# Layer two of an attention and mixture-of-experts kernel: how routing steps are let in between the products

## The chip, the cores and the metric

The kernel runs on one core of a Trainium2 chip. The metric is the time of one execution in device microseconds (us). A core has TensorE (PE, matrix products), VectorE (DVE), ScalarE (ACT), GpSimd (POOL), and the queue of SyncE (SP), which issues most transfers. Each engine takes its own instructions in order; between engines only semaphores order the work.

## The reference

Three stages follow each other, all in fp32. Stage one is attention (4 batches, 8 heads, 768 positions, 64 wide). Stage two sends each of 3072 tokens that a skip score keeps to its best of 8 experts. Stage three, called layer two here, is the one that the change touches:

```python
cap = N // E                                  # 3072 // 8 = 384
logits = x @ w_gate
for idx in np.argsort(-logits.flatten()):     # best pairs first
    tok, e = idx // E, idx % E
    if assigned[tok] >= 0 or counts[e] >= cap:
        continue
    assigned[tok] = e
    counts[e] += 1
for e in range(E):
    mask = assigned == e
    out[mask] = np.maximum(x[mask] @ w1[e], 0.0) @ w2[e]
```

So every expert gets 384 tokens, and which ones depends on which experts were full before.

## The kernel before, in words

**Products.** Layer two has eight units, one per expert, in the order in which the experts fill up. A unit works through 8 chunks of its 1024 hidden columns. Operands are split into a high and a low half (`xh`, `xl`, `wh`, `wl`, `h` twice), so that a chunk is 12 matmuls `ph` (128x384) and 9 matmuls `py` (128x512), 1344 in all. `wh` is written by ScalarE from the raw weights `wr` (four buffers, filled by SP), `wl` by POOL in four steps of 128x256, or by VectorE in one of 128x1024.

**Routing.** `phase` (line 1731) finds which expert fills next and which tokens it takes. It searches the threshold in 7 digits. For each digit VectorE compares all scores (`gm`), TensorE counts (`pr<-oh,gm`), and VectorE reads the digit off the counts. A count has two forms: the direct one (24 matmuls, then `fl,wt`) and the grouped one (six matmuls, a cast `cs`, then one or four sum matmuls with `sel` or `sels`; the last digit uses `identh` and `fl,wt`). Then follow `c,tri`, `ttb,tri`, `part,ones` and three `tb_rhs,mp`, each after VectorE operations; the last give the token numbers `ids`. With these POOL gathers the rows of the next unit (three gathers `xg`), TensorE turns them (`ident,xg`), ScalarE writes `xh` and VectorE `xl`. SP reads the expert's number `ei` and loads its weights.

**What sets the order.** The program is written out once, with a planner beside it. `Clock` (line 20) keeps a planned time for each engine; `cost` (line 76) says how long an operation is planned to take, and `ready` when an operand is planned to be there. The routing and the turns are generators (`Stream`, line 1211). Before each product `hook` (line 1240) lets a stream take its next step if `when()` is not later than the planned TensorE time plus `T_EPS`; `wait_for` (line 1258) steps the streams when there are no products, with matmuls on fixed data (`ph<-ones,tri`) as fill. The planner's numbers thus decide how many products stand between two routing steps in TensorE's queue, and nothing else: at run time the queues simply run.

**The start of layer two** (lines 2016 to 2034). Unit 0's rows are gathered in three blocks; `do_load` (line 508) puts a tiny write into the weight buffer ahead of each of four loads (the gate), so that the load can't start before that write has its turn. Meanwhile the fill runs, and phase 1 is already under way. `direct` (line 1757) says which digits are counted in the direct form, numbering them through the phases: the first 13.

Of the kernel before, what the change touches and what calls it, by code (L numbers as in the profile page):

```python
# [12 lines left out]
AF = mybir.ActivationFunctionType  # L13
# [6 lines left out]
class Clock:  # L20
# [4 lines left out]
    def __init__(self):  # L25
        self.at = dict.fromkeys(("pe", "dve", "act", "pool", "sp", "dma"), 0.0)
        self.seen, self.slots, self.count, self.log = {}, {}, {}, {}
        self.on = False
        self.late, self.fine = 0, False

    def place(self, t):
        if t.name not in self.slots:
# [43 lines left out]
    def cost(self, eng, op, outs, ins, extra):  # L76
        n = max([1] + [a.free_size() for a in outs[:1] + ins])
        if eng == "pe":
            d = str(ins[-1].dtype)
            n = outs[0].free_size()  # L80
            if op == "matmul" and d.endswith("float32") and ins[0].free_size() == 32 and outs[0].start_partition():
                n = 8
            if d.endswith("float32r") and ins[0].free_size() == 128:
                n = max(n, 250)
            return max(0.027, n * (2 if op == "transpose" else 4 if d.endswith("float32") else 1) / 2400.0)
        if eng == "dve":
            one = op in ("tensor_copy", "tensor_scalar", "memset") and all(a.tensor.space != "PSUM" for a in ins) and n % 2 == 0
            return 0.067 + 0.06 * extra + n / (1920.0 if one else 960.0)
        if eng == "act":
            return (0.051 if any("PSUM" in str(a.tensor.space) for a in ins) else 0.094) + n / 1200.0  # L90
        if op == "indirect_dma_start":
            return 1.038
        return 0.036 + n * (0.0022 if op == "tensor_tensor" else 0.0011)
# [77 lines left out]
def tile_attn_moe_moe(ctx: ExitStack, tc: tile.TileContext, q, k, v, n_global, n_local,  # L171
                      w_skip, w_gate, w1, w2, w2_gate, w21, w22, out):
    nc = Chip(tc.nc)
# [45 lines left out]
    pcol = sm.tile([128, 1], F32, name="pcol")  # L219
# [229 lines left out]
    class Weights:  # L449
# [58 lines left out]
        def do_load(self, i):  # L508
            c = self.order[i]
            u, j = divmod(c, NCH)  # L510
            t = wraw.tile([128, 1024], F32, name="wr")
            a = self.src[u][0 if j < 4 else 1]
            if self.gate:
                nc.vector.memset(t[0:1, 0:1], 0.0)
            if j < 4 and u in self.by_cols:
                nc.sync.dma_start(t.rearrange("p (c f) -> p c f", c=KC),
                                  a(0, Dm).rearrange("(c p) f -> p c f", p=128)[:, :, j * 256:(j + 1) * 256])
            elif j < 4:
                nc.sync.dma_start(t, a(j * 128, 128))
            else:  # L520
                nc.sync.dma_start(t.rearrange("p (c d) -> p c d", c=2),
                                  a((j - 4) * 256, 256).rearrange("(c p) d -> p c d", p=128))
            self.raw[c] = t
            self.loaded += 1
# [33 lines left out]
    WWT, WWN = 1, (2, 5)  # L558
    T_GAP, T_SP, T_EPS, T_W, T_P, T_L, T_F, X_B, T_H, T_M, LEAN, T_G, DIRECT, CUT = 0, 0.65, 0.1, 0, 8, 1, 0.3, 3, -4, 0, 2, 1, 13, 16
    T_LOW = 0.7  # L560
    LATE = 0.3
    PAUSE = 1
    T_U = 0.15
    ck.late = 2.0
# [293 lines left out]
    for g in range(-3, NU + 1):  # L858
# [16 lines left out]
        m, t = divmod(g + 4, NG)  # L875
# [35 lines left out]
    class Unit:  # L911
        at, tb, py, defer, xh, x2, turns, third, banks = None, 0, 0, None, None, None, False, False, None
        n = [128] * (CAP // 128)
# [294 lines left out]
    unit_no = [0]  # L1208
    result = {}

    class Stream:
# [12 lines left out]
        def when(self):  # L1224
            eng, aps = self.need
            if eng == "pt":
                t = ck.ready("pe", last_pt, aps)
                return max(t, ck.at["dve"] + T_LOW) if lows else t
            t = ck.ready(eng, (), aps)
            return max(t, ck.at["dve"] - T_SP) if eng == "dve" else t  # L1230

    streams = []
    held_back = []

    def order():
        free = [s_ for s_ in streams if not s_.busy]
        now = [s_ for s_ in free if not (s_.kind in held_back and s_.need[0] == "dve")]
        return sorted(now or free, key=lambda s_: s_.rank())
# [12 lines left out]
    def warm(until):  # L1251

        if ck.at["pe"] + 0.11 <= until:
            p = fps.tile([128, 512], F32, name="ph", bufs=2)
            while ck.at["pe"] + 0.11 <= until:
                nc.tensor.matmul(p[:, :256].rearrange("p (a n) -> p a n", a=2), tri, wide_one, start=True, stop=True)

    def wait_for(over, fill=False):
        while not over():
            t = min(s_.when() for s_ in order()) + T_F  # L1260
            s_ = next(s_ for s_ in order() if s_.when() <= t)
            if unit_no[0] < 0 and s_.kind == "main":
                first_ = min((o for o in order() if o.kind != "main"), key=lambda o: o.when(), default=None)
                if first_ and first_.when() < s_.when() + T_M:
                    s_ = first_
            if fill and s_.need[0] != "dve":
                warm(s_.when() - T_U)
            s_.step()
# [225 lines left out]
    BITS = ((27, 32), (22, 32), (17, 32), (12, 32), (7, 32), (2, 32), (0, 4))  # L1494
# [236 lines left out]
    def phase(ph_):  # L1731
# [7 lines left out]
        mb = m[:, :, None]  # L1739
        for it, (s_, n_) in enumerate(() if last else BITS):  # L1740
            if it and any(s_.kind == 'x' for s_ in streams):
                yield "dve", ()
            gm_ = rt.tile([128, NT * 32], BF, name="gm")
            gm = gm_[:, :NT * n_].rearrange("p (t n) -> p t n", n=n_)
            cut = {0: [CUT], 1: [2 * NT // 3]}.get(ph_, [])
# [7 lines left out]
            if it:  # L1753
                dv.tensor_tensor(nx[:, 0, :nn], tb_[:, :nn], thr[:, 0:1].to_broadcast([128, nn]),
                                 op=OP.bitwise_xor)
            low = it + 1 == len(BITS)
            direct = ph_ * len(BITS) + it < DIRECT
            wide = not direct and not low
            cnt = fps.tile([128, 2, 64], F32, name="pr")[:, 0, :CG * E]
            if direct:  # L1760
# [57 lines left out]
        else:  # L1818
            dv.scalar_tensor_tensor(fo[:, 0], pn_, v_[:, 1:2], first, op0=OP.is_equal, op1=OP.mult)
        dv.tensor_reduce(fx[:, 0:1], fo[:, 0], axis=AX.X, op=OP.max)  # L1820
        wait_for(lambda: not [s_ for s_ in streams if s_.kind == "ids"])
        yield "dve", ()
        fe = rt.tile([128, 6, NT], F32, name="fe", bufs=2)
        if not last:
            ts_ = thr.bitcast(F32)
# [90 lines left out]
    def routing():  # L1916
        yield from table_rows(units1[E - 1])
        for p in range(E):
            yield from phase(p)
# [74 lines left out]
    units2 = []  # L1994
# [21 lines left out]
    held_back.clear()  # L2016
    ck.late = LATE
    units2[0].banks = ("pt", "py1", "py2")
# [2 lines left out]
    split_next()  # L2021
    W_.gate = True
    for tb in range(1, NH):
        wait_for(lambda: units2[0].tb == tb, True)
        W_.limit = W_.limit + 1 if tb + 1 < NH else None
        W_.preload()
    W_.gate = False
# [38 lines left out]
```

## Time and profile before

| | before |
|---|---|
| median of 3 runs (lowest, highest) | 775.62 us (775.53, 776.88) |
| the profiled execution: time, span | 777.47 us, 775.7 us |
| TensorE busy in the span | 744.8 us (96%) |
| VectorE, ScalarE, POOL busy | 526.1, 403.3, 468.2 us |
| granted TensorE clock | 0.997 |
| stages: attention, layer one, start of layer two, layer two, end | 264.6, 185.9, 14.1, 305.6, 5.5 us |

The stages were cut at the first and last product of each. Busy time is that of the intervals in which an engine had an instruction in work. The end of a matmul is modelled in the profile, so rows of TensorE are read by their starts: from the start of one to the start of the next. The numbers in brackets behind a row of a timeline are the idle time of that engine ahead of it, and what ended it.

### The profile page before, as it was taken

Reading aid. Unit: us, or ns where it says so; the run is one execution under the profiler, and the core shown is the slowest. Engines: PE = TensorE matmul, PEld = TensorE weight load, DVE = VectorE, ACT = ScalarE, POOL = GpSimd, SP = SyncE. Lnnn points to the kernel's source line nnn. Section 1 sums busy time; section 2 is a strip of 40 time slices with the busy share of each in tenths; the row PEclk is TensorE's granted clock in tenths of the full one; section 3 lists DMA queues with packets and bytes.
Section 4 is the critical chain, followed back from the end, with each engine's and each line's share of the span. In section 5 each row is a group of like instructions: output and inputs, shape, how many; then the busy total and the mean of one; then the engine's idle time right before and its main releaser. Section 6 shows DMA issues by size and latency. Waiting matters only on the chain.

```text
span 775.7 us, 17432 instructions
## 1 busy us (share of the span) xinstructions
PE 744.8 (96%) x5910; PEld 628.7 (81%) x5910; DVE 526.1 (68%) x1952; ACT 403.3 (52%) x936; POOL 468.2 (60%) x821
## 2 busy tenths in 40 slices
PE   7999999899889999999999999999999999999997
PEld 5887777677659999999888677878788878788986
DVE  5987988979556676777634586778787778752110
ACT  5887787887547655555652113434333434255221
POOL 4664456755214464555793636975768777689911
PEclk9999999999999999999999999999999999999999
DMA  8686988897716766777760035626262636366311
GB/s 192 167 213 167 248 232 200 222 231 199 236 27 213 265 198 195 252 234 224 210 220 33 19 91 191 209 91 222 77 204 84 230 108 206 125 195 185 121 41 41
DMA packets 145370, 132.23 MB, mean 170 GB/s; under 512 B 65427, under 2 KB 112787, under 8 KB 145280
## 3 DMA queue, kind: packets, MB, share of 16 engines
q1 hardware_dynamic: 136896, 111.19, 48.9%
q0 software_dynamic: 6784, 19.51, 7.4%
q8 instruction: 48, 0.79, 0.4%
q10 hardware_dynamic: 1600, 0.39, 0.2%
q14 instruction: 42, 0.34, 0.1%
HBM read 108.80 MB, written 22.79 MB: 170 GB/s over the span
## 4 chain that ended last, share of the span: by engine, by line
PE 44%; POOL 8%; issue 6%; DMA 5%; DVE 4%; ACT 3%; POOLq 0%; DVEq 0%; ACTq 0%; SPq 0%
PE py L132 19%; PE ph L132 19%; POOL wl L132 7%; DMA wr<-in_moe_w_dram 4%; PE pr L132 3%; PE pt L132 3%; ACT wh L132 2%; DVE wl L132 1%; POOL out_dram L132 1%; DMA xg<-x2d,ids 1%; DVE py L132 1%; ACT ya L132 0%; DVE h L132 0%; POOL xg L132 0%; DVE o L132 0%
## 5 line engine op out<-in xcount | busy, mean ns | idle before, releaser
L132 POOL TENSOR_TENSOR wl<-wr,wh 128x256 fp32r<-128x256 f32 x356 | 253.6, 745 | 62.0 <-ACT wh L132 61.3
L132 ACT ACTIVATE wh<-wr 128x1024 fp32r<-128x1024 f32 (+1 forms) x148 | 142.2, 985 | 42.8 <-DMA wr<-in_moe_w_dram 26.8
L132 PE MATMUL py<-wh,h 128*128 128x512 f32 (+1 forms) x448 | 155.9, 401 | 0.0
L132 ACT ACTIVATE h<-ph 128x208 fp32r<-128x208 f32 (+2 forms) x132 | 54.4, 415 | 180.7 <-PE ph L132 168.3
L132 POOL TENSOR_SCALAR pb<-pb,st 128x232 f32<-128x232 f32 (+1 forms) x192 | 83.4, 453 | 74.3 <-ACT pb L132 24.2
L132 ACT ACTIVATE pb<-sb,st 128x232 f32<-128x232 f32 (+1 forms) x192 | 113.8, 664 | 10.1 <-DVE st L132 9.8
L132 DVE SCALAR_TENSOR_TENSOR h<-ph,h 128x208 fp32r<-128x208 f32 (+1 forms) x128 | 58.8, 460 | 88.8 <-ACT h L132 88.7
L132 PE MATMUL ph<-xh,wh 128*128 128x208 f32 (+1 forms) x512 | 99.1, 310 | 1.4 <-DVE h L132 1.4
L132 PE MATMUL ph<-xh,wl 128*128 128x208 f32 (+1 forms) x512 | 100.0, 311 | 0.0
L132 PE MATMUL ph<-xl,wh 128*128 128x208 f32 (+1 forms) x512 | 99.0, 311 | 0.0
L132 PEld LDWEIGHTS py<-wh,h 128*128 128x128 f32 (+1 forms) x448 | 82.0, 185 | 14.1
L132 PE MATMUL py<-wl,h 128*128 128x512 f32 (+1 forms) x224 | 90.9, 406 | 0.0
L132 PEld LDWEIGHTS ph<-xh,wh 128*128 128x128 f32 x512 | 82.2, 190 | 6.8 <-DVE h L132 1.6
L132 PEld LDWEIGHTS ph<-xl,wh 128*128 128x128 f32 x512 | 78.9, 190 | 1.1 <-issue 1.0
L132 PEld LDWEIGHTS ph<-xh,wl 128*128 128x128 f32 x512 | 78.9, 190 | 0.5 <-issue 0.3
L132 DVE TENSOR_TENSOR wl<-wr,wh 128x1024 fp32r<-128x1024 f32 x47 | 61.0, 1304 | 15.3 <-ACT wh L132 15.2
L132 DVE CUSTOM_DVE_ANT_0 sb<-pS,bias 128x232 f32<-128x232 f32 (+1 forms) x192 | 61.4, 374 | 8.9 <-PE pS L132 7.6
L132 DVE COPY pts<-pP 116x512 f32<-116x512 f32 (+1 forms) x96 | 60.7, 672 | 7.6 <-PE pP L132 7.1
L132 POOL DMA_INDIRECT xg<-x2d,ids x24 | 23.8, 990 | 52.2 <-DVE ids L132 19.1
L132 PE MATMUL pS<-kt,qt 64*128 64x232 f32 (+1 forms) x384 | 50.7, 382 | 1.0 <-ACT pb L132 1.0
L132 PE MATMUL pP<-ident,pb 128*116 128x128 f32 (+1 forms) x384 | 51.3, 277 | 0.0
L132 PE MATMUL pO<-pts,vw 116*64 116x128 f32 x640 | 46.3, 281 | 4.0 <-DVE pts L132 3.2
(465 smaller groups left out, 1267.5 us busy)
## 6 DMA issues: line engine op xcount, KB each, us to landing
wr<-in_moe_w_dram SPq DMA_DIRECT2D x136, 512.0 KB
xd<-xs SPq DMA_DIRECT2D x32, 192.0 KB
x2d<-xs SPq DMA_DIRECT2D x32, 192.0 KB
kraw<-in_k_dram SPq DMA_DIRECT2D x30, 192.0 KB
qraw<-in_q_dram SPq DMA_DIRECT2D x30, 192.0 KB
vw<-in_v_dram SPq DMA_DIRECT2D x32, 160.0 KB
vw<-in_v_dram SPq DMA_DIRECT2D x32, 120.0 KB
xT<-in_moe_w_dram SPq DMA_DIRECT2D x1, 1536.0 KB
```

The lines of the kernel that those rows point to most:

```text
L132: r = f(*a, **k)
```

## The change

It is made of seven small edits, all of which bear on layer two alone, but for one term of the planner's cost.

- `Clock.cost`: in layer two a product is planned 0.016 us longer, and a matmul of over 0.1 us that follows one of under 0.06 us gets 0.085 us more (this one also in layer one).
- `do_load`: the tiny gate write moves from VectorE (a 1x1 memset) to ScalarE (a 1x1 activation). On ScalarE one of the four stands ahead of the second `xh` of unit 0, three ahead of the third.
- `LATE` 0.3 becomes 0: unit 0's gathers are planned to land that much earlier.
- `when`: two new kinds of need. `gm` is ready 0.1 us before the planned VectorE time; `ids` waits until no stream of kind `ids` runs.
- `phase`: a digit is let in by `gm` where a turn is under way; and a `wait_for` that ran other streams on the spot becomes a `yield` of `ids`.
- `direct`: direct form only until the first product of layer two (unit number still negative), grouped from then on.
- the wait between unit 0's gated loads asks how many blocks have been turned (line 1112), not how many have their `xl` too.

```diff
-        self.late, self.fine = 0, False
+        self.late, self.fine, self.short = 0, False, False
...
-            return max(0.027, n * (2 if op == "transpose" else 4 if d.endswith("float32") else 1) / 2400.0)
+            t = (0.016 if self.fine and d.endswith('float32r') else 0) + max(0.027, n * (2 if op == "transpose" else 4 if d.endswith("float32") else 1) / 2400.0)
+            back, self.short = self.short and t > 0.1, t < 0.06
+            return t + (0.085 if back else 0)
...
             if self.gate:
-                nc.vector.memset(t[0:1, 0:1], 0.0)
+                nc.scalar.activation(t[0:1, 0:1], pcol[0:1], AF.Copy)
...
-    LATE = 0.3
+    LATE = 0.0
...
+            if eng == "gm":
+                return ck.at["dve"] - 0.1
+            if eng == "ids":
+                return 1e9 if [s_ for s_ in streams if s_.kind == "ids"] else ck.at["dve"] - T_SP
...
             if it and any(s_.kind == 'x' for s_ in streams):
-                yield "dve", ()
+                yield "gm", ()
...
-            direct = ph_ * len(BITS) + it < DIRECT
+            direct = unit_no[0] < 0
...
-        wait_for(lambda: not [s_ for s_ in streams if s_.kind == "ids"])
-        yield "dve", ()
+        yield "ids", ()
...
-        wait_for(lambda: units2[0].tb == tb, True)
+        wait_for(lambda: len(units2[0].xt) >= tb, True)
```

What this does to the queues is seen in the order of instructions. (Line 132, after the change 134, is a helper that records every operation.) The direct counts fall from 288 to 192 matmuls, that is from 12 to 8; four become grouped, with 24 more matmuls of the grouped sort and 16 more with `sels`. On VectorE 47 operations `wl` become 46, on POOL 356 become 360.

First place: TensorE's queue at the start of layer two, around the third turn of unit 0 (`ident,xg`). Before, it stands inside a direct count (`oh,gm`):

```order
L132 LDWEIGHTS gm
L132 MATMUL pr<-oh,gm 32x8
L132 LDWEIGHTS gm
L132 MATMUL pr<-oh,gm 32x8
L132 MATMUL py_7784<-ident,xg_7600 128x128 x4
L132 LDWEIGHTS gm
L132 MATMUL pr<-oh,gm 32x8
L132 LDWEIGHTS gm
L132 MATMUL pr<-oh,gm 32x8
```

After, it stands in the fill (`ones,tri`):

```order
L134 MATMUL ph<-ones,tri 128x256
L134 MATMUL py_7756<-ident,xg_7598 128x128 x4
L134 LDWEIGHTS tri
L134 MATMUL ph<-ones,tri 128x256
L134 LDWEIGHTS tri
```

and the same count comes only behind the first product (`ph<-xh,wh`):

```order
L134 LDWEIGHTS tri
L134 MATMUL ph<-ones,tri 128x256
L134 MATMUL ph<-xh,wh 128x384
L134 LDWEIGHTS gm
L134 MATMUL pr<-oh,gm 32x8
```

The third turn and the count have changed places, and the first product has moved ahead of the count.

Second place: TensorE's queue in phase 3, from `fl,wt`, which closes the last digit, to `c,tri`, which sums the tokens above the threshold (`c` is written by VectorE). Before:

```order
L132 LDWEIGHTS wt
L132 MATMUL pr<-fl,wt 128x8
L132 MATMUL py_9125<-wh,h_9122 128x512
L132 MATMUL py_9126<-wh,h_9122 128x512
L132 MATMUL py_9126<-wl,h_9122 128x512
L132 MATMUL py_9126<-wh,h_9122 128x512
L132 MATMUL ph<-xh,wh 128x384 x4
L132 MATMUL ph<-xl,wh 128x384 x3
L132 LDWEIGHTS tri_4461
L132 MATMUL pr<-c_9213,tri_4461 128x1
L132 LDWEIGHTS tri
L132 MATMUL pr<-c_9213,tri 128x1
```

After:

```order
L134 LDWEIGHTS wt
L134 MATMUL pr<-fl,wt 128x8
L134 MATMUL py_8525<-wl,h_8982 128x512
L134 MATMUL py_8525<-wh,h_8982 128x512
L134 MATMUL ph<-xh,wh 128x384 x4
L134 MATMUL ph<-xl,wh 128x384 x4
L134 LDWEIGHTS tri_4461
L134 MATMUL pr<-c_9106,tri_4461 128x1
L134 LDWEIGHTS tri
L134 MATMUL pr<-c_9106,tri 128x1
```

Four `py` and seven `ph` stood between the two; two `py` and eight `ph` stand there now.

Third place: the same queue a little later in phase 3, from `ttb,tri` to the first of the matmuls with `mp` (loaded from `mp`, which VectorE writes). Before:

```order
L132 MATMUL pt<-ttb,tri 128x1
L132 MATMUL py_9125<-wl,h_9174 128x512
L132 MATMUL py_9125<-wh,h_9174 128x512
L132 MATMUL py_9126<-wh,h_9174 128x512
L132 MATMUL py_9126<-wl,h_9174 128x512
L132 LDWEIGHTS ones
L132 MATMUL pr<-part,ones 128x8
L132 MATMUL py_9126<-wh,h_9174 128x512
L132 MATMUL ph<-xh,wh 128x384 x4
L132 MATMUL ph<-xl,wh 128x384 x4
L132 MATMUL ph<-xh,wl 128x384 x3
L132 LDWEIGHTS mp
```

After:

```order
L134 MATMUL pt<-ttb,tri 128x1
L134 MATMUL py_9165<-wl,h_9065 128x512
L134 MATMUL py_9165<-wh,h_9065 128x512
L134 MATMUL py_9166<-wh,h_9065 128x512
L134 LDWEIGHTS ones
L134 MATMUL pr<-part,ones 128x8
L134 MATMUL py_9166<-wl,h_9065 128x512
L134 MATMUL py_9166<-wh,h_9065 128x512
L134 MATMUL ph<-xh,wh 128x384 x4
L134 MATMUL ph<-xl,wh 128x384 x4
L134 LDWEIGHTS mp
L134 MATMUL pt<-tb_rhs,mp 128x27
```

Five `py` and eleven `ph` stood between; five `py` and eight `ph` stand there now. On POOL, unit 1's gathers stand behind 36 steps `wl` of the stage, where they stood behind 32.

## Rows read from the trace of the kernel before

**Rows 1.** Table by stages, layer two (columns: stretch, busy us and count by engine, clock).

```profile
464.57:770.20 305.63, 303.82 (x1853) 256.12 (x1851) 187.66 (x761) 118.17 (x171) 215.21 (x312) 1.00 0.45 146
```

**Rows 2.** What TensorE waited for, 464 to 755 us.

```profile
PE pt L132 <- DMA xg<-x2d,ids: 1.3, 2, 0.7
PE pr L132 <- DVE gm L132: 0.5, 1, 0.5
```

**Rows 3.** Timeline, TensorE, phase 3 (columns: start us, length us, engine, operation, count).

```profile
558.78 0.40 PE L132 MATMUL py<-wl,h 128*128 128x512 f32 x1
559.11 0.17 PE L132 MATMUL pr<-fl,wt 4*128 4x8 bf16 x1
559.22 0.73 PE L132 MATMUL py<-wh,h 128*128 128x512 f32 x2
...
561.55 0.19 PE L132 MATMUL pr<-c,tri 128*128 128x1 bf16 x2
561.61 0.42 PE L132 MATMUL ph<-xl,wh 128*128 128x384 f32 x1
561.86 0.86 PE L132 MATMUL ph<-xh,wl 128*128 128x384 f32 x4
562.56 0.39 PE L132 MATMUL py<-wh,h 128*128 128x512 f32 x1
...
563.49 0.18 PE L132 MATMUL pt<-ttb,tri 128*128 128x1 bf16 x1
...
566.83 0.24 PE L132 MATMUL pt<-tb_rhs,mp 128*128 128x27 bf16 x3
```

**Rows 4.** Timeline, VectorE, phase 3.

```profile
561.34 0.15 DVE L132 TENSOR_REDUCE c<-fe 128x2 bf16<-128x2 f32 x1
...
564.66 0.55 DVE L132 SCALAR_TENSOR_TENSOR h<-ph,h 128x384 fp32r<-128x384 f32 x1
...
566.17 0.60 DVE L132 SCALAR_TENSOR_TENSOR mp<-islot,fx,pt 128x384 bf16<-128x384 f32 x1
```

**Rows 5.** Timeline, TensorE, start of layer two.

```profile
461.70 0.60 PE L132 MATMUL py<-ident,xg 128*128 128x128 f32 x4
...
462.75 0.56 PE L132 MATMUL pr<-oh,gm 128*32 128x8 bf16 x16
463.23 0.66 PE L132 MATMUL py<-ident,xg 128*128 128x128 f32 x4
...
464.57 0.62 PE L132 MATMUL ph<-xh,wh 128*128 128x384 f32 x2
```

**Rows 6.** Timeline, ScalarE, the first weight split of layer two.

```profile
468.12 1.06 ACT L132 ACTIVATE wh<-wr 128x1024 fp32r<-128x1024 f32 x1 [3.60 <-DMA wr<-in_moe_w_dram]
```

**Rows 7.** Timeline, TensorE, a direct count between products.

```profile
466.38 0.51 PE L132 MATMUL ph<-xh,wl 128*128 128x384 f32 x2
466.82 0.76 PE L132 MATMUL pr<-oh,gm 128*32 128x8 bf16 x24
467.51 0.62 PE L132 MATMUL ph<-xh,wl 128*128 128x384 f32 x2
```

**Rows 8.** Timeline, TensorE, a grouped count between products.

```profile
502.09 0.51 PE L132 MATMUL ph<-xl,wh 128*128 128x384 f32 x2
502.44 0.32 PE L132 MATMUL pr<-oh,gm 128*128 128x32 bf16 x6
502.61 0.60 PE L132 MATMUL ph<-xl,wh 128*128 128x384 f32 x2
```

**Rows 9.** Timeline, POOL, around unit 1's gathers.

```profile
488.42 2.83 POOL L132 TENSOR_TENSOR wl<-wr,wh 128x256 fp32r<-128x256 f32 x4
492.38 1.70 POOL L132 DMA_INDIRECT xg<-x2d,ids  x1 [1.13 <-DMA wr<-in_moe_w_dram]
494.39 0.95 POOL L132 DMA_INDIRECT xg<-x2d,ids  x1 [0.30 <-issue]
```

**Rows 10.** Timeline, VectorE, beside unit 1's first gather.

```profile
492.03 1.23 DVE L132 TENSOR_TENSOR wl<-wr,wh 128x1024 fp32r<-128x1024 f32 x1
```

## The prediction

> **What bounds the kernel now.** I read the table by stages first [rows 1]: in layer two (464.57 to 770.20 us) TensorE is busy 303.82 of 305.63 us at the full granted clock, so that stage ends when TensorE has got through its queue, and only what makes that queue longer, later or idle counts. Then the waits [rows 2]: TensorE stands idle 1.3 us for gathered rows and 0.5 us for one `gm`, nothing else the profile puts a name to. So the change has to be priced as TensorE time: the start of the first product, small matmuls put between the products, and stalls at the small matmuls that wait for VectorE.
>
> The products are 12 `ph` and 9 `py` matmuls for each of 64 chunks. A `ph` step is 0.175 us (four from 561.86 to 562.56), a `py` step 0.232 us (four from 562.56 to 563.49) [rows 3]. What an inserted step costs is the time from the product before it to the product after it, less the product steps between. For `fl,wt`: 558.78 to 559.22 less one `py` is 0.21 us [rows 3].
>
> The row that matters most is the one that doesn't look like a wait. After `fl,wt` at 559.11 TensorE reaches `c,tri` at 561.55, 2.44 us later; the products there (four `py`, seven `ph`) and the 0.21 make 2.36, so it stood 0.08 us [rows 3]. VectorE writes `c` at 561.34 for 0.15 us, thus until 561.49 [rows 4]: the chain from `wt` to `c` takes all of the 2.44. Each of the six phases that run beside products shows the same 2.44 of need. The same holds from `ttb,tri` (563.49) to `tb_rhs,mp` (566.83) [rows 3]: the second `mp` operation ends at 566.77 [rows 4]. Of these 3.34 us about 0.45 go to an `h` operation of the products that landed inside the chain at 564.66 [rows 4]; without one the need is about 2.9.
>
> **The change part by part.**
>
> *The start.* Before, the third turn of unit 0 (463.23) stands behind sixteen compare matmuls that begin only at 462.75, and the first product follows 1.34 us after it, at 464.57 [rows 5]. Afterwards the turn stands ahead of the next compare, so it can go as soon as its rows are there, right behind the second turn (461.70) and its fill, from about 462.1 on, and the first product from 463.5. Against that stand the new 1x1 ScalarE operations: one ahead of the second `xh`, three ahead of the third. The trace shows no such operation; bounds are 0 (they run while ScalarE waits for the turn) and 0.6 us (four of the smallest VectorE operations here, 0.15 each [rows 4], all in the way). The start gains 0 to 1.1 us; I take 0.6. The gates also let unit 0's next weights go earlier: `wh` at 468.12 waits 3.60 us for its transfer [rows 6], and `h` of chunk 0, its compare and the 0.5 us wait for `gm` hang on that. The one-line change of the first-unit wait serves the same end and is priced with it. The four VectorE memsets that go stood in nobody's way.
>
> *Grouped instead of direct.* A direct count of 24 matmuls costs 466.38 to 467.51 less two `ph`, 0.78 us [rows 7]; with its `fl,wt` 0.99. The grouped six cost 502.09 to 502.61 less two `ph`, 0.17 us [rows 8], and their four sum matmuls, of which no row stands here, between 0.12 (four at the rate of the `c,tri` pair, 561.55 to 561.61) and 0.21 (as much as `fl,wt`) [rows 3]; I take 0.17, so 0.34. Before, four direct iterations lie between products, one with the 0.5 us stall: 4 x 0.99 + 0.5 = 4.5. Afterwards one direct iteration and four grouped: 0.99 + 4 x 0.34 = 2.4. Gain 2.1 us (1.9 to 2.3).
>
> *The planner's clock.* The steps of the routing are let in when the planned TensorE clock passes the planned VectorE time. A product now counts 0.016 us more, near what the trace shows, so fewer products lie between two routing steps: by the order of instructions 10 or 8 in place of 12 or 11. VectorE's chain is as long as it was. From `wt` to `c,tri` phase 3 now has two `py` and eight `ph`: 0.46 + 1.40 + 0.21 = 2.07 us, against 2.44 of need: a stall of 0.37 where 0.08 was. The six phases have 2.01 to 2.12: 6 x 0.37 less about 0.45 in all before is +1.8. From `ttb,tri` to `mp` phases 1 to 4 now have 2.4 to 2.7 us, the 0.1 of the steps themselves included, against 2.9: stalls of 0.5, 0.5, 0.2, 0.5 where about 0.2 each stood (phase 3: five `py` and eleven `ph`, 3.09 of the 3.34): +0.9; phases 5 and 6 about +0.1. From `c,tri` to `ttb,tri`, 1.7 to 2.0 against 1.94 (the row of phase 3, nothing between) or 0.5 more with an `h`: +0.2. From `sels` to the next compare the distances are 2.2 to 2.6, near their need: +0.3. Sum +3.3. The lower bound is the 1.8 of `wt` to `c` alone, where no `h` takes part; the upper is 4.6, with `h` operations inside three of the chains (0.45 each). Routing ends earlier, in unit 4 in place of unit 5; that gives nothing to TensorE, since it removes no step.
>
> *Gathers.* The 1.3 us of [rows 2] are unit 1's first turn and unit 7's. Unit 1's gather took 1.70 us where its neighbours take 0.95 [rows 9], beside a VectorE `wl` of 1.23 us [rows 10]. Afterwards that `wl` is POOL's: four steps, 2.83 us for four [rows 9], ahead of the gather. So the gather may start later by up to 2.8 less what it gained from earlier routing, and unit 7's, which now stands behind fewer `wl`, may lose its stall. Bounds +1.0 and -1.3, taken as 0, since the two go in opposite ways by like amounts.
>
> The Trainium skill, page "GPSIMD Engine Reference", section "Key points", says that GpSimd shares its SBUF interfaces with VectorE and is slowed by VectorE operations with two SBUF inputs. `wl` on VectorE is one, and the 1.70 against 0.95 agrees. By that rule alone the move of this `wl` to POOL would give the gather its 0.75 us back and the forecast would be 775.4; the four steps ahead of it are what the rule leaves out.
>
> *Sum.* -0.6 - 2.1 + 3.3 + 0 = +0.6 us. The profiled execution took 777.47 us (span 775.7), 1.85 above the runs' median of 775.62; its durations thus give 778.1, and on the scale of the median 776.2. About 0.2% (1.55 us) is what a measurement of this kernel can tell from no change, so the likeliest result is no change, 776.2 us; its own range, from the bounds most likely to meet, is 774.1 to 777.2.
>
> **Rivals.** *VectorE is not as late as I reckon* (faster). For it: the need was read where products left it just that long; where an `h` operation falls outside the chain or the six waits come down to `wt` to `c` alone, the planner costs 1.8, and unit 7's stall goes: -0.6 - 2.1 + 1.8 - 0.9 = -1.8, 773.8 us. Against: six phases with one and the same 2.44. Chance 0.31.
>
> *The chains catch an `h` operation* (slower). With fewer products between the steps, a chain of VectorE and the `h` of the running chunk meet as they did at 564.66 [rows 4], now with no slack behind. Price 4.6 in place of 3.3, and the start gains nothing because the three ScalarE gates hold the third `xh`: 0 - 2.1 + 4.6 + 0 = +2.5, 778.1 us. It decides from two such meetings on (0.9 us) together with a lost start. Against: both have to come together, and the `wt` to `c` chain of phase 3 met none. Chance 0.34.
>
> *The change does half of what it says* (no change): grouped form as priced, but `wh` still waits for its transfer since the gate's ScalarE operation stands behind the `xh` before it; then the start gives 0 and the sum is +1.2, 776.8 us. It is part of the no-change case, with my forecast together 0.35.
>
> **How the numbers follow.** Faster by over 0.2% 0.31, within 0.35, slower 0.34. Ends: all bounds low (-1.1 - 2.3 + 1.8 - 1.3 = -2.9) gives 772.7, all high (0 - 1.9 + 4.6 + 1.0 = +3.7) gives 779.3; either end needs four things at once, so I cut to 773.2 and 778.8, which leaves about 2 in 10 outside.
>
> **What would show it.** In the profile after: the first product near 464.0 and the first `wh` of the stage no longer at 468.12; no wait for `gm` of 0.5 us at unit 0; waits of TensorE of 0.3 to 0.4 us on VectorE's `c` in each phase and of 0.2 to 0.5 on `mp`; the excess of the six grouped counts at 0.17. I am wrong if the waits for `c` and `mp` don't appear (then the need was no need, and the time is near 774), or if the gathers of units 1 to 7 show waits of over 1 us, which I have at nothing.

## The result and the profile after

The changed kernel takes 781.95 us (780.1 to 785.82 in seven runs), before 775.62: ratio 1.0083, 95% interval 1.0057 to 1.0108, about 6.4 us slower. I had forecast 776.2 us in 773.2 to 778.8, and slower by over 0.2% with 0.34. The direction came out as my slower rival's, at a price beyond my range.

First the ends of the stages, read from starts of products in the two timelines:

| us | before | after |
|---|---|---|
| last product of layer one | 450.29 | 448.71 |
| from it to the first of layer two | 14.29 | 13.18 |
| first to last product of layer two | 305.58 | 311.84 |

Ahead of 448.71 the change touches only the planning of a few steps of layer one; the 1.6 us there were already apart at the first product of layer one (235.40 and 233.81). The clock shows why: from 232.2 to 235.5 the granted clock was 0.50 in the profiled execution before and 1.00 in that after, and half of 3.3 us is 1.65. It is about as much as the 1.85 us by which the profiled execution of before lay above its median. So the spans differ by 3.5 us only (775.7 and 779.2), and the change itself by -1.1 + 6.3 = +5.2. The rest up to 6.4 lies in runs that no profile shows; two of the seven took over 785 us with a mean granted clock of 0.99.

The table by stages, after (answers to [rows 1]):

```profile
461.89:774.00 312.11, 308.57 (x1815) 255.25 (x1815) 188.56 (x775) 118.44 (x171) 217.51 (x316) 1.00 0.44 143
```

What TensorE waited for from 461 to 765 us, after (answers to [rows 2]; total, times, longest):

```profile
PE pr L134 <- DVE ei L134: 0.9, 4, 0.3
PE pt L134 <- DVE ttb L134: 0.5, 1, 0.5
PE pt L134 <- DVE mp L134: 0.5, 2, 0.3
PE pr L134 <- DVE part L134: 0.3, 2, 0.2
PE pt L134 <- DMA xg<-x2d,ids: 0.2, 1, 0.2
PE pr L134 <- DVE c L134: 0.2, 1, 0.2
```

The routing steps have taken the place of the gather and the `gm` (the `ei` is written beside `c` and is `c,tri`'s wait). But the view adds up to 2.6 us. A wait shows there only where the modelled end of the matmul before is past; the starts show all of it. TensorE, phase 3, after (answers to [rows 3]):

```profile
548.41 0.17 PE L134 MATMUL pr<-fl,wt 4*128 4x8 bf16 x1
...
549.07 0.87 PE L134 MATMUL ph<-xh,wh 128*128 128x384 f32 x4
549.78 0.87 PE L134 MATMUL ph<-xl,wh 128*128 128x384 f32 x4
550.85 0.19 PE L134 MATMUL pr<-c,tri 128*128 128x1 bf16 x2 [0.20 <-DVE c L134]
...
552.73 0.16 PE L134 MATMUL pt<-ttb,tri 128*128 128x1 bf16 x1
...
553.69 0.17 PE L134 MATMUL pr<-part,ones 128*128 128x8 bf16 x1
...
554.98 0.87 PE L134 MATMUL ph<-xl,wh 128*128 128x384 f32 x4
556.13 0.24 PE L134 MATMUL pt<-tb_rhs,mp 128*128 128x27 bf16 x3 [0.28 <-DVE mp L134]
...
561.04 0.32 PE L134 MATMUL pr<-oh,gm 128*128 128x32 bf16 x6
```

VectorE there (answers to [rows 4]):

```profile
550.64 0.15 DVE L134 TENSOR_REDUCE c<-fe 128x2 bf16<-128x2 f32 x1
...
553.96 0.55 DVE L134 SCALAR_TENSOR_TENSOR h<-ph,h 128x384 fp32r<-128x384 f32 x1
...
555.47 0.60 DVE L134 SCALAR_TENSOR_TENSOR mp<-islot,fx,pt 128x384 bf16<-128x384 f32 x1
...
560.03 0.95 DVE L134 TENSOR_TENSOR gm<-m,py 128x768 bf16<-128x768 f32 x1
```

From `wt` to `c,tri` it is 2.44 us again, with fewer products in between: four `ph` from 549.78 would have ended the wait at 550.48, and `c,tri` starts at 550.85. The same stands before `mp`, which comes 0.45 behind the eighth `ph`. The next compare follows the end of `gm` (560.98) by 0.06, but here TensorE got to it only 0.02 us too early; in the other phases this compare stood 0.08 to 0.19 us. Worked out in this way for all 1343 steps between products, and summed by what stands between them:

| us beyond the product steps (times) | before | after |
|---|---|---|
| `c,tri` | 0.7 (6) | 2.5 (6) |
| `ttb,tri` and `part,ones` | 0.6 | 2.9 |
| `tb_rhs,mp` | 0.9 (7) | 2.7 (7) |
| grouped counts | 6.8 (35) | 9.3 (40) |
| `sel` and `sels` | 1.0 (23) | 2.3 (29) |
| direct counts | 3.7 (4) | 0.9 (1) |
| `fl,wt` | 2.2 (11) | 1.4 (7) |
| turns | 10.2 | 10.1 |

The start, TensorE and ScalarE, after (answers to [rows 5] and [rows 6]):

```profile
459.41 0.60 PE L134 MATMUL py<-ident,xg 128*128 128x128 f32 x4
...
460.61 0.60 PE L134 MATMUL py<-ident,xg 128*128 128x128 f32 x4
...
461.89 0.44 PE L134 MATMUL ph<-xh,wh 128*128 128x384 f32 x1
```

```profile
459.44 0.19 ACT L134 ACTIVATE wr<-pcol 1x1 f32<-1x1 f32 x1
...
460.54 0.37 ACT L134 ACTIVATE wr<-pcol 1x1 f32<-1x1 f32 x3
461.24 0.60 ACT L134 ACTIVATE xh<-py 128x512 fp32r<-128x512 f32 x1 [0.33 <-PE py L134]
463.79 1.06 ACT L134 ACTIVATE wh<-wr 128x1024 fp32r<-128x1024 f32 x1 [1.95 <-DMA wr<-in_moe_w_dram]
```

The third turn goes at 460.61 and the first product 1.28 us behind it. The three gates take 0.37 us together, and ScalarE still waits 0.33 us for the turn: they hold nobody. A grouped count's four `sels`, in unit 0 after (answers to [rows 8]):

```profile
466.22 0.70 PE L134 MATMUL ph<-xl,wh 128*128 128x384 f32 x3
466.77 0.26 PE L134 MATMUL pr<-cs,sels 128*128 128x8 f16 x4
466.88 0.42 PE L134 MATMUL ph<-xl,wh 128*128 128x384 f32 x1
```

0.66 less three `ph` is 0.14 us, where I took 0.17; the four such sums of unit 0 average 0.18.

### The profile page after: what moved, and what is told of

Read it like the earlier page. It is cut to its first block, busy times and chain, and to the rows that moved or that the text cites. A ratio compares the mean times of both kernels' runs of the same rounds, so it can differ in the third digit from the quotient of the medians.

```text
span 779.2 us, 17316 instructions
## 1 busy us (share of the span) xinstructions
PE 747.7 (96%) x5847; PEld 625.8 (80%) x5847; DVE 526.2 (68%) x1963; ACT 404.3 (52%) x940; POOL 468.5 (60%) x825
## 4 chain that ended last, share of the span: by engine, by line
PE 44%; DVE 10%; issue 6%; POOL 3%; DMA 3%; ACT 3%; POOLq 0%; SPq 0%; DVEq 0%; ACTq 0%
PE ph L134 19%; PE py L134 19%; PE pr L134 4%; PE pt L134 3%; DMA wr<-in_moe_w_dram 3%; POOL wl L134 2%; DVE py L134 2%; ACT wh L134 2%; DVE wl L134 1%; POOL out_dram L134 1%; DVE h L134 1%; DVE fe L134 1%; DMA xg<-x2d,ids 1%; DVE fx L134 1%; DVE pt L134 0%
## 5 line engine op out<-in xcount | busy, mean ns | idle before, releaser
L134 PE MATMUL py<-wh,h 128*128 128x512 f32 (+1 forms) x448 | 157.6, 403 | 0.0
L134 ACT ACTIVATE pb<-sb,st 128x232 f32<-128x232 f32 (+1 forms) x192 | 113.8, 664 | 10.2 <-DVE st L134 9.7
L134 PEld LDWEIGHTS pO<-pts,vw 116*64 116x64 f32 x640 | 34.2, 136 | 16.2 <-ACT pb L134 6.6
```

Of the source, the lines that this page charges most:

```text
L134: r = f(*a, **k)
```

## The experiments

Ratios are to the kernel before on the same chip. Theory A: the planner's TensorE terms let routing steps reach TensorE before VectorE has their operands. Rival B: the new needs `gm` and `ids`; C: the start and the grouped form; others as they came up.

**e1, the cost alone.**

```diff
+            t = (0.016 if self.fine and d.endswith('float32r') else 0) + max(0.027, ...)
...
+            return t + (0.085 if back else 0)
```

> The kernel before with the planner's TensorE cost alone changed (0.016 us more for a product, 0.085 us more behind a short matmul); everything else as before. Theory A (the planned TensorE clock runs faster while VectorE's planned chain stays short, so TensorE reaches c,tri, ttb,tri, part,ones, mp and the next compare before VectorE has them): by the order, the products between wt and c,tri are worth 1.85 to 2.08 us, between ttb,tri and mp 2.0 to 2.5 us; the stalls of the changed kernel come nearly in full, +6 to +8 us, 781.5 to 783.5 us. Rival B (the new needs gm and ids, or the earlier gathers, cost the time): 775.6 within 1 us. Rival C (the start and the grouped form cost the time): the same, 775.6.

786.26 us, ratio 1.0108 (1.0088 to 1.0128). Theory A holds, and the size, +8.4 us, is a little over its +6 to +8: this one edit alone is at least as slow as all seven together. B and C fall as the main cause. But then the other six must gain:

**e2, all but the cost.** The same lines taken out of the changed kernel.

> The changed kernel with the planner's TensorE cost as it was before; all other edits in. Theory A: the distances are back at those of before (wt to c,tri 2.1 to 2.25 us of products, ttb,tri to mp 2.5 to 3.1), so no new stalls; what is left is the start (-1.1) and the grouped form (-2.0): 772.5 us, 771.5 to 773.5. Rivals B and C: as slow as the changed kernel, 780 to 782 us.

778.75 us, 1.0024 (1.0010 to 1.0038). The stalls are gone (`c,tri` 0.7, `mp` 1.0 us, as before), yet the 3 us of gain didn't come: a miss. Most is lost in one place: unit 1 takes 42.2 us, 38.7 before (a unit is counted here as 168 products, see the table at the end). TensorE's list of waits has 1.8 us for `gm` and 0.7 for `xh`.

**e3, VectorE planned slower too.**

```diff
-            return 0.067 + 0.06 * extra + n / (1920.0 if one else 960.0)
+            return 0.067 + (0.05 if self.fine else 0) + 0.06 * extra + n / (1920.0 if one else 960.0)
```

> The changed kernel with 0.05 us more for each VectorE operation in the planner's cost (in layer two alone), so that both sides of the comparison are near what the trace shows. By the order the products between wt and c,tri are worth 2.32 to 2.43 us (with 0.2 for the wt step more than the need of 2.44), between c,tri and ttb,tri 2.26 to 2.37, between ttb,tri and mp 2.7 to 2.8. Theory A: no stalls at these steps, not even the 1 to 1.5 us of the kernel before; start and grouped form stay: 771 to 772.5 us. Rival B: 779 to 782 us. A theory D, that TensorE loses by the number of short matmuls and not by waiting, expects no change against the changed kernel, 780 to 782.

787.61 us, 1.0142 (1.0114 to 1.0171). A miss that taught most. The stalls at the steps went (`c,tri` 0.4 and `mp` 0.75 us in all), as A wants, and D falls with that, since as many short matmuls stand there as in the changed kernel; but the waits of TensorE are now others:

```profile
PE pt L134 <- DMA xg<-x2d,ids: 7.4, 7, 2.0
PE pt L134 <- issue: 2.4, 1, 2.4
PE pr L134 <- DVE gm L134: 0.8, 2, 0.7
...
```

Routing that is let in later ends later, and the next unit's rows are not there when their turns stand in the queue.

**e4, the grouped form alone.**

```diff
-            direct = ph_ * len(BITS) + it < DIRECT
+            direct = unit_no[0] < 0
```

> The kernel before with the rule for the direct form alone changed (direct only until the first product of layer two). My term of the prediction was -2.1 us: four direct counts between products (0.99 each and a 0.5 us wait) become grouped ones at 0.34. Expected 773.5 us, 773.0 to 774.5. If the grouped form's longer chain through VectorE (cast, sum, transpose) eats the gain: 775.6.

780.94 us, 1.0048 (1.0031 to 1.0065): slower by 3.7 where I had it faster by 2.1. TensorE from the end of unit 0 to the first product of unit 1 (505.03):

```profile
500.30 0.40 PE L132 MATMUL py<-wh,h 128*128 128x512 f32 x1
501.63 0.31 PE L132 MATMUL pr<-oh,gm 128*128 128x32 bf16 x6 [0.93 <-DVE gm L132]
503.08 0.18 PE L132 MATMUL pr<-cs,sel 128*128 128x32 f16 x1 [1.14 <-DVE cs L132]
503.68 0.66 PE L132 MATMUL pt<-ident,xg 128*128 128x128 f32 x4 [0.42 <-DVE xl L132]
505.03 1.33 PE L132 MATMUL ph<-xh,wh 128*128 128x384 f32 x3 [0.69 <-ACT xh L132]
```

The grouped form takes TensorE's time out of unit 0, not VectorE's time out of phase 1. So unit 0's products run out before unit 1 is ready, its third turn stands behind a count of phase 2, and 3.2 us of waits follow. They cost more than themselves (same kernel, table by stretches; after POOL's column the granted clock):

```profile
490.00:500.00 10.00, 9.40 (x57) 8.15 (x56) 8.24 (x27) 2.88 (x6) 3.59 (x3) 1.00 0.80 268
500.00:505.00 5.00, 1.84 (x15) 0.88 (x13) 4.76 (x16) 1.98 (x4) 0.00 (x0) 0.97 0.13 29
505.00:508.50 3.50, 3.47 (x16) 2.86 (x17) 2.52 (x11) 0.92 (x1) 2.50 (x4) 0.50 0.29 109
508.50:512.00 3.50, 3.50 (x14) 2.84 (x13) 1.78 (x4) 1.09 (x2) 0.28 (x1) 0.56 0.48 150
512.00:520.00 8.00, 7.55 (x54) 6.10 (x54) 5.67 (x26) 5.37 (x7) 5.18 (x8) 1.00 0.01 3
```

Behind a hole in which TensorE was busy 1.84 of 5 us, the products run at the lower clock (0.50, that is 1.2 GHz) until about 511.5. This leads to theory F: the grouped form pays only if phase 1 becomes faster as well, and in the changed kernel that is what the cost edit does there.

**e5, VectorE planned slower from phase 2 on.**

```diff
+            return 0.067 + self.slow + 0.06 * extra + n / (1920.0 if one else 960.0)
...
+        ck.slow = 0.05 if ph_ >= 2 else 0.0
...
-    ck.late, ck.fine = 0.5, True
+    ck.late, ck.fine = 1.2, True
```

> The changed kernel with 0.05 us more for a VectorE operation in the planner's cost, but from phase 2 of the routing on (phase 1 stays as changed), and gathers planned to land 1.2 us later than their issue's cost in place of 0.5. By the order phase 1 keeps its short distances; phases 2 to 6 have 2.3 to 2.5 us of products between wt and c,tri, 2.2 to 2.4 from c,tri to ttb,tri, 2.7 to 2.8 from ttb,tri to mp, so nothing waits there. Theory A (stalls at the routing steps, 6 us in five phases): it loses them, keeps the start (-1.1) and the grouped form (-2.0), and is some 3 us under the kernel before, ratio 0.996. A theory E, that what counts is when the rows of the next unit come (the first kernel with slow VectorE was 10 us slower, with a hole of 4.2 us at unit 1 and turns that waited 7.4 us): the later routing makes turns wait again, 3 to 6 us over the kernel before, ratio 1.004 to 1.008.

779.66 us, 1.0039 (1.0023 to 1.0056), at the low end of what E says. Units 0 to 2 take 41.7, 38.6 and 38.9 us, about as good as any kernel here, so A is right there; unit 5 takes 41.0 (37.1 before), with a hole ahead of unit 6, so E is right there.

**e6, without the 0.085 us.**

```diff
-            return t + (0.085 if back else 0)
+            return t
```

> The changed kernel without the 0.085 us behind a short matmul, with the 0.016 us for a product. By the order the sum of the six distances from wt to c,tri is 12.0 us (11.2 in the changed kernel, 13.2 before), from ttb,tri to mp in the middle too. Theory A, with a stall for what is missing: about 60% of the changed kernel's loss at the routing steps, 2 us under it: ratio to the kernel before 1.005 to 1.006. If the 0.016 were all: 1.008; if the 0.085 were all: 0.997.

780.2 us, 1.0034 (1.0019 to 1.0048): under the 1.005 expected, but between the two ends; both terms take part. In the profile `c,tri` costs 1.6 us (2.5 with both, 0.7 before), in step with the distance. But the time isn't these stalls alone: the profile also has a wait of 1.6 us for `xh` ahead of unit 1 and products at a granted clock of 0.50 from 505.4 to 508.7.

**e7, the needs of before.** `when`, `gm` and `ids` taken back.

> The changed kernel with the needs of before (no gm, no ids: a digit waits for the planned VectorE time, and the streams of kind ids are run on the spot). Theory A: the distances are as short (11.6 us from wt to c,tri in sum), so it is as slow as the changed kernel, ratio 1.007 to 1.010. Rival B (the new needs cost the time): 0.997 to 1.000.

785.26 us, 1.0102 (1.0081 to 1.0124). Rival B falls.

**e8, the start alone.**

```diff
-                nc.vector.memset(t[0:1, 0:1], 0.0)
+                nc.scalar.activation(t[0:1, 0:1], pcol[0:1], AF.Copy)
...
-    LATE = 0.3
+    LATE = 0.0
...
-        wait_for(lambda: units2[0].tb == tb, True)
+        wait_for(lambda: len(units2[0].xt) >= tb, True)
```

> The kernel before with the ScalarE gates, the first-unit wait and LATE at 0 alone. The order keeps the direct counts (their places between products move from 10, 25, 34, 44 to 13, 24, 32, 42) and the distances of phases 1 to 6. My term was -0.6 us (0 to -1.1); the changed kernel's first product came 1.1 us earlier after the last of layer one. Expected -1.1 us: ratio 0.9986. If the start is given back at unit 1: 1.000.

776.23 us, 0.9989 (0.9977 to 1.0000): -0.9 us, with an interval that reaches zero. The size is within my term of -0.6 (0 to -1.1), the place is not. In the profile the third turn (463.09) now stands ahead of the count, but the count (464.13) still stands ahead of the first product, which follows the last of layer one by 14.16 us (14.29 before). What it saves is the wait of 0.5 us for `gm`: the direct count that cost 1.33 us costs 0.78.

**e9, the cost in phase 1 only.** The new terms hold until phase 2 of the routing begins.

```diff
+            t = (0.016 if self.fine and self.tight and d.endswith('float32r') else 0) + max(0.027, ...)
+            return t + (0.085 if back and self.tight else 0)
...
+        ck.tight = ph_ < 2
```

> The changed kernel, but with the planner's new TensorE terms (0.016 and 0.085 us) only until phase 1 of the routing is done; from phase 2 on products are planned as before. By the order phase 1 is as in the changed kernel, phases 2 to 6 have the distances of the kernel before (2.1 to 2.25 us from wt to c,tri). Theory A with F (the grouped form shortens unit 0, and only a faster phase 1 brings unit 1's rows early enough to keep that): start -1.1, unit 0 -1.3 to -2, units 1 to 6 as before: ratio to the kernel before 0.996 to 0.997. If the routing steps of phases 2 to 6 are not where the changed kernel loses: 1.006 to 1.008.

774.13 us, 0.9972 (0.9959 to 0.9985): faster than both kernels, by 2.2 us against before. TensorE's waits in layer two:

```profile
PE pt L135 <- DMA xg<-x2d,ids: 1.1, 1, 1.1
PE pr L135 <- DVE ei L135: 0.3, 1, 0.3
```

**e10, the mirror:** `ck.tight = ph_ != 1`.

> The mirror of the one before: the new TensorE terms only from phase 2 of the routing on, phase 1 planned as before, all other edits in. Theories A and F: a hole before unit 1 as in the kernel with all edits but the cost (+4 us in unit 1) and the stalls of phases 2 to 6 (+7.6 us in units 1 to 6 less what phase 1 had): ratio 1.009 to 1.013, the slowest of the mixtures. Without F it would be as the changed kernel, 1.007 to 1.008.

789.87 us, 1.0176 (1.0155 to 1.0197), above the 1.013 expected. Unit 0 takes 47.1 us: the hole is that of e4, with 2.0 us of wait for one `cs`, and it was followed by products at the lower clock, 0.50 from 506 to 512. I had left that price out.

**e11, as e9 with the direct form.**

> As the first of these four, with the direct form as before (the first 13 digits). It tells what the grouped form is worth where unit 1's rows come early: my term of the prediction was 2.1 us, so 2 us over the first of these four, ratio 0.999. If grouped and direct are worth the same once VectorE's chain sets phase 1: the same as the first, 0.996 to 0.997.

776.36 us, 1.0001 (0.9990 to 1.0012). Against e9 the grouped form is worth 2.2 us (2.9 in the profiles, 306.82 and 303.97 us from first to last product): my term of 2.1, where unit 1 is ready.

**e12, as e5 with 0.03 us.**

> The changed kernel with 0.03 us more (0.05 in the run before) for a VectorE operation in the planner's cost from phase 2 on, gathers planned to land 1.2 us late. By the order the turns of unit 6 stand at products 905 to 925 (983 to 999 with 0.05, where unit 6 begins at 1008), so its hole of 5 us in units 5 and 6 goes; the distances are still those at which nothing waits (2.1 to 2.3 us from wt to c,tri). Theory A with F: ratio 0.995 to 0.997, at or under the first of these four. If slower routing costs in any case: 1.002 to 1.004.

776.14 us, 0.9994 (0.9982 to 1.0006). The hole ahead of unit 6 is gone (unit 5 takes 36.0 us), but turns wait 3.8 us in two places, and unit 4 takes 43.0. Expected 0.995 to 0.997: a miss. Slower planning of VectorE takes the stalls away and gives waits for rows back.

The lengths of the units show all of it. A unit is counted here as 168 products, from the start of one to the start of the 168th after it; the first nine `ph` of the next unit mostly come ahead of the last nine `py`, so a hole ahead of unit 1 falls into the figure for unit 0 (in e2 into that for unit 1):

| us, units 0 to 6 | |
|---|---|
| before | 43.8, 38.7, 39.1, 38.6, 39.2, 37.1, 35.7 |
| after | 42.5, 41.0, 42.4, 41.6, 41.2, 34.8, 35.0 |
| e2, all but the cost | 42.4, 42.2, 38.8, 39.1, 38.7, 37.6, 35.8 |
| e4, grouped alone | 46.5, 41.1, 38.7, 39.2, 38.7, 37.3, 36.1 |
| e9, cost in phase 1 | 41.7, 38.7, 39.1, 38.7, 39.2, 37.0, 36.0 |
| e10, the mirror | 47.1, 43.5, 42.2, 41.5, 41.6, 34.8, 35.0 |

After, units 1 to 4 carry five phases of routing with their stalls, +10.6 us; units 5 and 6 get 3.0 back, since routing is over by then.

## Why the prediction was wrong

**The mechanism was right, one term was too small.** The step that failed is *The planner's clock*, "Sum +3.3", upper bound 4.6. Measured against before, step by step:

- `wt` to `c,tri`: +1.8 forecast, +1.8 measured. Here the need was constant and I had it in every phase.
- `ttb,tri` over `part,ones` to `mp`: "+0.9" and 0.1 forecast, +1.2 (`part`) and +1.8 (`mp`) measured. I took 0.2 of stall per phase as standing there before and so subtracted, for four phases, what mostly was the steps' own cost; and I let `part,ones` pass as part of the way to `mp`, though it has its own need: in phase 3 `part` was read 0.96 us after `ttb,tri` with three `py` (0.69) between. Phases 5 and 6, which I had at 0.1, give 1.1 of it: there `part,ones` follows `c,tri` directly, 2.30 us behind it, with products for 1.85.
- `c,tri` to `ttb,tri`: +0.2 forecast, +1.0 measured. I took 1.94 from phase 3; in three of the six phases it is 2.15. And 0.6 of it is one step of phase 6, where TensorE comes to `ttb,tri` from `part,ones` (654.52, 659.45) and stands.
- `mp` to the first compare of the next phase: not priced at all, +0.6 measured over five phases. It is the longest chain of all: VectorE works without pause from `mp` (555.47) to `gm` (560.98), and before the change TensorE came to the compare 0.5 to 0.7 us after `gm` was done.
- `sel` or `sels` to the next compare: +0.3 forecast, +1.0 measured (the grouped counts inside the phases, beyond the 0.17 or 0.33 us that they cost before).
- A compare to its `sel`, by way of `cs`: not priced, +0.5 measured.

That is 7.9 where I had 3.3. The lesson in the working: I priced the pair that was easiest to see, and bounded the others by half a microsecond each, when the right bound was the whole chain. From `fl,wt` to the next compare the chain needs 2.4 + 2.2 + 2.9 + 5.0 = 12.5 us (12.4 to 12.9 in phases 1 to 4 after the change); the products planned there after the change are worth 1.85 + 1.9 + 2.3 + 4.7 = 10.8, before 2.15 + 1.9 + 2.9 + 6.0 = 13.

**The start** came at its upper bound in the profile, -1.1, and the reason was right (the turn ahead of the count); ScalarE's gates cost nothing. But it isn't a gain of its own: the first product is earlier because a direct count that stood ahead of it (0.89 us) now stands behind it. My sum is right with this, since it has that count in the next term. e11, with this start and the direct form (and the cost in phase 1), shows it: its first product comes 1.1 us earlier and layer two is 1.2 us longer, 1.0001 in all. What e8 gained is the wait for `gm`, which I had in the next term too.

**Grouped instead of direct** was right in size (2.2 us in e9 against e11) and wrong as a gain by itself: alone it loses 3.7. I counted TensorE's time in unit 0 and not who sets its end. In the changed kernel the two edits meet well: the cost edit hurries phase 1, unit 1 is ready, no hole comes. That is also why taking the cost out gives back 4.6 us only (1.0083 to 1.0024) and not 7.9.

**Gathers at 0** was right in sum: the turns cost 10.2 and 10.1 us. Unit 1's first `wl` did go to POOL and stands ahead of the gathers (four steps from 487.27), as I said, and so did unit 2's. The first gather begins 2.1 us earlier all the same (490.24), of which 1.6 are the stages before: the earlier routing made up for the four steps. What I didn't see, and what makes my 0 luck in part, is that VectorE took unit 1's second `wl` instead (491.66); it begins after the gather that it meets and cost it nothing.

**The rivals.** "VectorE is not as late as I reckon" falls: e3 lengthened the distances and the stalls vanished. "The chains catch an `h`" was the right side with the wrong mechanism: the one `h` at 553.96 was there before as well; the stalls need none. "Half of what it says" falls: `wh` came 4.3 us earlier, of which 1.6 are the stages before and 1.1 the start. A rival I lacked: the new order is good in phase 1 and bad in the five phases after it, with a sum on either side of zero.

**The forecast's scale.** I subtracted 1.85 us between profile and median; the stages show that 1.6 of it sat ahead of layer two, with the lower clock from 232.2 to 235.5, so it was right to do so.

## What to carry to other kernels

A planner compares two clocks; when one is corrected with measured durations and the other isn't, the error that cancelled shows, and here 0.016 us per product and 0.085 behind a short matmul became nearly 8 us of stalls. Correcting the other too took the stalls away but made rows late (e3, e12). So price such an edit by the whole chain between two hand-overs, every link of it, and by starts, since a list of waits misses those under the modelled end of the instruction before. And time taken from one engine is only won where what comes next is ready: a change may need its partner (a faster phase 1) in one stage and be spoiled by the same partner in the others.

## What the runs showed of the hardware

**A gather behind VectorE's `wl` waits for its end.** Before, the gather issued 0.35 us into a `wl` took 1.70 [rows 9, 10]. After, the one beside it began 0.16 us ahead of the `wl` and took 0.95:

```profile
490.24 0.95 POOL L134 DMA_INDIRECT xg<-x2d,ids  x1
491.50 0.95 POOL L134 DMA_INDIRECT xg<-x2d,ids  x1 [0.30 <-issue]
492.75 0.95 POOL L134 DMA_INDIRECT xg<-x2d,ids  x1 [0.30 <-issue]
```

```profile
491.66 1.22 DVE L134 TENSOR_TENSOR wl<-wr,wh 128x1024 fp32r<-128x1024 f32 x1
```

The one at 492.75 began 0.13 us ahead of the end of the `wl` and took 0.95 as well. In e9 one began 0.81 us into a `wl` of 1.22 and took 1.23. What was left of the `wl`, plus 0.82 us, is the gather's time in these (0.88 + 0.82, 0.13 + 0.82, 0.41 + 0.82). In layer one of the changed kernel eleven gathers and scatters begin inside a `wl`, and took what was left of it plus 0.79 to 0.91 us, at most 1.94 us (at 283.16, 0.17 us into one). The Trainium skill, "GPSIMD Engine Reference", section "Key points", names contention with VectorE operations that have two SBUF inputs; these rows agree and say how: it is the start of the gather that decides, and the price is what is left of the `wl`, not a share of every overlap.

**The price of a hole.** In e4 TensorE was busy 1.84 of 5 us, in e10 3.37 of 6 us, and then its granted clock was 0.50 for 6 us or so in which it had work nearly all the time. By the steps from product to product there this cost 2.8 and 2.4 us more, nearly as much again as the waits (3.2 and 3.3). e3 has the same hole and the same low clock. e2 has smaller waits in the same place (0.4, 0.7 and 0.3 us, then 1.5), and its clock stayed at 1.00, as it did in the changed kernel, whose stalls at the routing steps are 0.6 us at most each.
